# Clock-keeping products into unread accumulator columns, small loads later, and a new order of steps, in an attention and gated-MLP kernel

## Chip, cores, metric

One core of a Trainium2 chip. The metric is the device time of one execution in microseconds (us), lower is better. Engines: PE is TensorE, PEld its weight loads, DVE VectorE, ACT ScalarE, POOL GpSimd, SP SyncE.

## The reference, cut to what matters

```python
# q, k, v: 4 batches, 8 heads, 768 positions, 64 wide
keep = is_sink(4 first keys) | (0 <= row - col < 128)
a = softmax(where(keep, q @ k.T / 8, -1e9))
x = heads side by side of a @ v                       # 4 x 768 x 512
h = gelu(x @ w_in); u, v = halves of h
v = (v - mean(v)) / sqrt(var(v) + 1e-6) * g_ln
out = x + (u * (w_sg @ v + b_sg)) @ w_out             # w_sg mixes positions
```

## The kernel before

A list of steps is worked off in order. A step records instructions for one engine; each engine runs its own in that order, and the recording layer adds the waits between engines. `TQ`, `TK` turn q and k on TensorE, `EQ`, `EK` copy them out of PSUM, `QK` makes scores, `EX` their exponentials, `MK` masks them, `AV` multiplies by v, `NR` normalizes; `XT`, `XE` turn x; `MU`, `MV` are the gated unit's two halves, `SP` the mixing over positions, `GT` and `GM` the gate, `OU`, `RA`, `ST` the output. Numbers are batch, head pair, part; a last letter names the engine (A, D, P). PSUM has two double buffers `sc` and four single ones `mm`, taken in turn.

```python
pre = [0]
def HM(n):                       # n constant products, before the next product
    pre[0] = n
def fresh(ring, key):
    t = ring.new(key)
    for _ in range(pre[0]):      # into the buffer just given out; result never read
        nc.tensor.matmul(t if ring is mm_ring else t[:, 0, :], iden, ks_sink[1][:, 0:512], ...)
    pre[0] = 0
    return t
def TQ(b, p):                    # by way of transposes(): fresh(mm_ring, ...), 12 turns into columns 0:384
    ...
def MK(b, p, g, e):              # D: P = P * mask on VectorE; P: two affine_selects on GpSimd
    ...
def GM(b, hf, dc, e):            # gate product on VectorE (D) or GpSimd (P), all in SBUF
    (nc.vector if e == "D" else nc.gpsimd).tensor_mul(gatedT[...], gtmp[b, hf, dc], uT[b][...])
```

The softmax here doesn't subtract the row's maximum and nothing guards it: scores larger than these inputs give would overflow.

Of the kernel before, what the change touches and what calls it, by code (L numbers as in the profile page):

```python
# [13 lines left out]


STEPS = """
ZERO IDEN LQ.0.0 LK.0.0 LQ.0.1 FILL LK.0.1 LC MASK LV.0.0 MASK0 CQ.0.0.A LQ.0.2 HM.7 TQ.0.0 CK.0.0.A LK.0.2 EQ.0.0.A
LV.0.1 HM.2 TK.0.0 TQ.0.1 EK.0.0.A VSK EQ.0.1.D LQ.0.3 HM.2 QK.0.0.1 QK.0.0.2 KS.0.0 EX.0.0.1 VSM.3 LK.0.3 TK.0.1
SK.0.0 LV.0.2 VSM.1 EK.0.1.D CV.0.0.P EX.0.0.2 HM.6 QK.0.0.0 MK.0.0.1.D LV.0.3 TQ.0.2 SX.0.0 QK.0.1.0 KS.0.1 EX.0.0.0
EQ.0.2.D TK.0.2 MK.0.0.2.P SK.0.1 EX.0.1.0 EK.0.2.D QK.0.1.1 LW.0 EX.0.1.1 MK.0.0.0 HM.1 QK.0.2.1 LW.1 KS.0.2 TQ.0.3  # L20
VSM.0 SX.0.1 QK.0.2.0 EQ.0.3.A LWS SK.0.2 MK.0.1.1.D TK.0.3 EX.0.2.1 AV.0.0.0 MK.0.1.0 LWO AV.0.0.1 EK.0.3.A NR.0.0.0
QK.0.2.2 MK.0.2.1.P SX.0.2 NR.0.0.1 EX.0.2.0 CV.0.2.D LQ.1.0 KS.0.3 EX.0.2.2 CV.0.3.D LK.1.0 HM.7 QK.0.3.0 SK.0.3
MK.0.2.0 EX.0.3.0 QK.0.3.1 LV.1.0 MK.0.2.2.D AV.0.2.0 EX.0.3.1 MK.0.3.0 QK.0.3.2 AV.0.2.1 CV.0.1.P NR.0.2.0 EX.0.3.2
QK.0.1.2 NR.0.2.1 SX.0.3 MK.0.3.1.P AV.0.1.0 EX.0.1.2 NR.0.1.0 MK.0.3.2.P HM.1 AV.0.3.0 XT.0.0 NR.0.3.0 MK.0.1.2.P
AV.0.3.1 XE.0.0.D XT.0.1 NR.0.3.1 LV.1.1 AV.0.1.1 XE.0.1.A VSM.2 XT.0.3 LQ.1.1 MU.0.0 XE.0.3.A NR.0.1.1 LK.1.1 XT.0.2
LV.1.2 GU.0.0 MV.0.0 LV.1.3 LG WT.1 LQ.2.0 XE.0.2.A WT.4 WE.1 WT.0 GV.0.0 LK.2.0 MV.0.1 WE.4 WE.0 BN.0.0 MV.0.2 GV.0.1
BN.0.1 MU.0.3 GV.0.2 TQ.1.0 BN.0.2 RS.0.1 GU.0.3 TQ.1.1 MU.0.2 EQ.1.0.A EQ.1.1.A NM.0.1 RS.0.2 TK.1.0 Z.0.0.A TK.1.1
Z.0.1.D Z.0.2.A WT.5 NM.0.2 CV.1.0.P EK.1.0.D MU.0.1 EK.1.1.A Z.0.4.D LV.2.0 GU.0.2 WE.5 WT.3 WT.2 Z.0.5.A CV.1.1.P
WE.3 QK.1.0.0 Z.0.3.A WE.2 LV.2.1 GU.0.1 SP.0.0.2 EX.1.0.0 LQ.2.1 TQ.1.2 GT.0.0.2 LK.2.1 SP.0.0.3 EQ.1.2.D GM.0.0.2.P
TK.1.3 GT.0.0.3 TQ.1.3 EK.1.3.A MK.1.0.0 TK.1.2 QK.1.1.0 EQ.1.3.A GM.0.0.3.D SP.0.0.0 CV.1.2.P EK.1.2.D EX.1.1.0  # L30
QK.1.1.1 CV.1.3.D LV.2.2 SP.0.1.1 EX.1.1.1 GT.0.0.0 MK.1.1.0 LV.2.3 QK.1.2.1 QK.1.2.2 MK.1.1.1.D SP.0.1.2 EX.1.2.1
LQ.3.0 KS.1.0 EX.1.2.2 LK.3.0 SP.0.0.1 GM.0.0.0.D GT.0.1.2 MK.1.2.1.P SK.1.0 GT.0.1.1 QK.1.1.2 GT.0.0.1 SX.1.0
QK.1.3.2 MK.1.2.2.P TK.2.0 EX.1.1.2 TK.2.1 AV.1.1.0 GM.0.1.2.D EK.2.0.A GM.0.0.1.D QK.1.0.1 NR.1.1.0 MK.1.1.2.P
AV.1.2.1 EK.2.1.A OU.0.0 EX.1.0.1 NR.1.2.1 CV.2.1.P AV.1.1.1 CV.2.0.A RA.0.0 MK.1.0.1.P SP.0.1.0 NR.1.1.1 EX.1.3.2
ST.0.0 LV.3.0 AV.1.0.0 GM.0.1.1.D MK.1.3.2.D TQ.2.2 QK.1.2.0 GT.0.1.0 LV.3.1 EQ.2.2.A QK.1.0.2 SP.0.1.3 NR.1.0.0
EX.1.2.0 GM.0.1.0.P XT.1.0 GT.0.1.3 EX.1.0.2 TK.2.3 MK.1.2.0 OU.0.2 XE.1.0.A MK.1.0.2.D EK.2.3.A AV.1.2.0 CV.2.2.P
RA.0.2 AV.1.0.1 NR.1.2.0 TQ.2.1 GM.0.1.3.P ST.0.2 TK.2.2 NR.1.0.1 EQ.2.1.A TQ.2.0 CV.2.3.P QK.1.3.1 EK.2.2.D EQ.2.0.A
QK.1.3.0 OU.0.3 LQ.3.1 EX.1.3.1 KS.2.0 LK.3.1 XT.1.2 EX.1.3.0 OU.0.5 RA.0.3 LV.3.2 MK.1.3.1.D ST.0.3 QK.2.1.1 XE.1.2.A
QK.2.1.2 LV.3.3 RA.0.5 TQ.2.3 EX.2.1.1 TK.3.1 MK.1.3.0 ST.0.5 AV.1.3.1 EX.2.1.2 EQ.2.3.D MK.2.1.1.P AV.1.3.0 QK.2.0.2
EK.3.1.A QK.2.0.0 NR.1.3.1 SK.2.0 CV.3.0.P EX.2.0.2 OU.0.1 NR.1.3.0 EX.2.0.0 MK.2.0.2.P XT.1.1 RA.0.1 QK.2.0.1 SX.2.0  # L40
QK.2.1.0 CV.3.1.P XE.1.1.D XT.1.3 EX.2.0.1 ST.0.1 OU.0.4 MK.2.1.2.D XE.1.3.A MK.2.0.0 MV.1.0 EX.2.1.0 MK.2.0.1.P
RA.0.4 ST.0.4 MK.2.1.0 AV.2.0.0 GV.1.0 MV.1.1 NR.2.0.0 TK.3.3 GV.1.1 TK.3.2 BN.1.0 TQ.3.2 TQ.3.3 EK.3.3.A MV.1.2
CV.3.2.P EQ.3.2.A EQ.3.3.D EK.3.2.A BN.1.1 CV.3.3.P MU.1.3 GV.1.2 AV.2.1.0 BN.1.2 GU.1.3 RS.1.1 MU.1.0 MU.1.1 GU.1.0
NM.1.1 RS.1.2 NR.2.1.0 Z.1.0.A Z.1.3.D MU.1.2 NM.1.2 Z.1.2.A Z.1.1.D Z.1.5.D GU.1.1 AV.2.1.1 Z.1.4.D GU.1.2 AV.2.0.1
NR.2.1.1 QK.2.3.1 QK.2.2.0 NR.2.0.1 SP.1.1.0 EX.2.3.1 SP.1.1.3 GT.1.1.0 GM.1.1.0.D SP.1.0.3 EX.2.2.0 GT.1.1.3
MK.2.3.1.P QK.2.3.0 GT.1.0.3 QK.2.2.1 SP.1.1.2 EX.2.3.0 GM.1.1.3.D GM.1.0.3.D MK.2.2.0 EX.2.2.1 SP.1.0.1 MK.2.3.0
SP.1.0.2 MK.2.2.1.P GT.1.1.2 GT.1.0.1 AV.2.3.0 GM.1.1.2.D QK.2.2.2 GT.1.0.2 GM.1.0.1.P QK.2.3.2 AV.2.2.0 EX.2.2.2
NR.2.3.0 SP.1.0.0 GM.1.0.2.P EX.2.3.2 NR.2.2.0 TQ.3.1 MK.2.2.2.P GT.1.0.0 XD.2.0 TK.3.0 EQ.3.1.A TQ.3.0 MK.2.3.2.D
AV.2.2.1 EK.3.0.A EQ.3.0.D GM.1.0.0.P QK.3.1.2 QK.3.1.1 EX.3.1.2 AV.2.3.1 NR.2.2.1 OU.1.1 EX.3.1.1 KS.3.0 QK.3.0.0
MK.3.1.2.P NR.2.3.1 QK.3.1.0 EX.3.0.0 OU.1.2 RA.1.1 XD.2.1 MK.3.1.1.D EX.3.1.0 OU.1.0 MK.3.0.0 QK.3.0.2 ST.1.1  # L50
QK.3.0.1 RA.1.0 EX.3.0.2 SK.3.0 SP.1.1.1 MK.3.1.0 ST.1.0 EX.3.0.1 RA.1.2 MK.3.0.2.P MU.2.1 SX.3.0 GT.1.1.1 ST.1.2
MK.3.0.1.D MV.2.0 GM.1.1.1.P GU.2.1 OU.1.4 GV.2.0 MV.2.1 RA.1.4 BN.2.0 ST.1.4 MV.2.2 GV.2.1 BN.2.1 MU.2.3 GV.2.2
OU.1.5 BN.2.2 RS.2.1 GU.2.3 MU.2.2 RA.1.5 RS.2.2 MU.2.0 GU.2.2 NM.2.1 ST.1.5 Z.2.2.D Z.2.0.A Z.2.3.D OU.1.3 Z.2.1.D
GU.2.0 NM.2.2 QK.3.2.1 Z.2.4.D Z.2.5.A QK.3.3.0 AV.3.1.0 RA.1.3 EX.3.3.0 AV.3.1.1 NR.3.1.0 ST.1.3 SP.2.0.2 NR.3.1.1
SP.2.1.3 GT.2.0.2 EX.3.2.1 MK.3.3.0 SP.2.1.1 GM.2.0.2.D MK.3.2.1.P GT.2.1.3 QK.3.2.0 GT.2.1.1 QK.3.3.1 EX.3.2.0
SP.2.0.0 GM.2.1.3.D GM.2.1.1.D EX.3.3.1 SP.2.0.3 MK.3.2.0 GT.2.0.0 MK.3.3.1.P AV.3.2.0 GT.2.0.3 AV.3.0.0 QK.3.2.2
NR.3.2.0 GM.2.0.3.P QK.3.3.2 AV.3.3.0 EX.3.2.2 NR.3.0.0 AV.3.0.1 EX.3.3.2 MK.3.2.2.P NR.3.3.0 SP.2.0.1 NR.3.0.1 XD.3.0
MK.3.3.2.P SP.2.1.0 GT.2.0.1 GM.2.0.0.D AV.3.2.1 GM.2.0.1.D AV.3.3.1 GT.2.1.0 OU.2.1 NR.3.2.1 GM.2.1.0.P NR.3.3.1
OU.2.2 RA.2.1 XD.3.1 OU.2.0 RA.2.2 SP.2.1.2 RA.2.0 ST.2.1 ST.2.2 ST.2.0 MU.3.0 GT.2.1.2 GM.2.1.2.P MV.3.0 GU.3.0
OU.2.4 GV.3.0 MV.3.1 RA.2.4 BN.3.0 ST.2.4 MV.3.2 GV.3.1 BN.3.1 OU.2.5 GV.3.2 MU.3.2 BN.3.2 RS.3.1 MU.3.1 GU.3.2 NM.3.1  # L60
RS.3.2 RA.2.5 Z.3.2.A MU.3.3 Z.3.0.D ST.2.5 Z.3.1.A NM.3.2 Z.3.3.D OU.2.3 Z.3.4.A Z.3.5.D GU.3.3 SP.3.1.0 RA.2.3
GU.3.1 ST.2.3 SP.3.1.3 GT.3.1.0 GM.3.1.0.P SP.3.0.0 GT.3.1.3 GM.3.1.3.D SP.3.0.2 GT.3.0.0 GM.3.0.0.D SP.3.1.1 GT.3.0.2
GM.3.0.2.D SP.3.1.2 GT.3.1.1 GM.3.1.1.P SP.3.0.3 GT.3.1.2 GM.3.1.2.D SP.3.0.1 GT.3.0.3 GM.3.0.3.P OU.3.5 GT.3.0.1
OU.3.3 GM.3.0.1.D RA.3.5 OU.3.2 RA.3.3 ST.3.5 OU.3.0 ST.3.3 RA.3.2 OU.3.4 ST.3.2 OU.3.1 RA.3.4 RA.3.0 ST.3.4 ST.3.0
RA.3.1 ST.3.1
"""


# [8 lines left out]
def kernel(  # L77
# [14 lines left out]
    nc = tc.nc  # L92
# [40 lines left out]
    mm_ring = Ring("mm", 4, [128, 512], F32, psum)  # L133
# [24 lines left out]
    ks_sink = [sb.tile([128, HP * (128 + ks_w)], BF16, name=f"ks_sink{i}") for i in range(2)]  # L158

    iden = sb.tile([128, 128], BF16, name="iden")  # L160
# [9 lines left out]
    b_bc = sb.tile([128, S], F32, name="b_bc")  # L170
# [2 lines left out]
    wsg_rows = wsg_gated.rearrange("p (t s) -> p t s", t=NT)  # L173
    gatedT = wsg_gated.rearrange("p (r c s) -> p r c s", r=3, c=KU)

    pre = [0]

    def HM(n):
        pre[0] = n

    def fresh(ring, key):
        t = ring.new(key)
        for _ in range(pre[0]):
            nc.tensor.matmul(t if ring is mm_ring else t[:, 0, :], iden, ks_sink[1][:, 0:512], start=True, stop=True)
        pre[0] = 0
        return t

    def psb(key):
        return mm_ring[key].bitcast(BF16)[:, 0:S].rearrange("p (t i) -> p t i", t=NT)
# [63 lines left out]
            nc.sync.dma_start(out=vs32[i:128:16, :, :], in_=v[:, :, i, :].rearrange("b h d -> h b d"))  # L253

    def LG():
        nc.sync.dma_start(out=g_sb, in_=moe_g_ln.rearrange("(c p) -> p c", p=128))
        return nc.sync.dma_start(out=b_bc, in_=moe_b_sg.partition_broadcast(128))


    def IDEN():  # L260
# [41 lines left out]
    def transposes(name, ring, b, p):  # L302
        src = ring[b, p // 2]
        fresh(mm_ring, (name, b, p))
        ps = psb((name, b, p))
        for t in range(NT):
            for hl in range(2):
                nc.tensor.transpose(ps[64 * hl:64 * hl + 64, t, :], src[:, 2 * (p % 2) + hl, t, :], iden)  # L308
# [221 lines left out]
    def ST(b, t):  # L530
        nc.sync.dma_start(out=out[b, 128 * t:128 * (t + 1), :], in_=ot[b, t])


    code = {f.__name__: f for f in (
        HM, LQ, LK, LV, CQ, CK, CV, LW, LWS, LWO, LC, LG, IDEN, FILL, MASK, MASK0, VSK, ZERO, VSM, TQ, TK, EQ, EK, KS, SK, SX, QK, EX,
        MK, AV, NR, XT, XE, XD, MV, GV, BN, RS, NM, Z, MU, GU, WT, WE, SP, GT, GM, OU, RA, ST)}
    holds = dict(h.split("<") for h in HOLDS.split())
# [43 lines left out]
```

## Time and profile before

| kernel before | value |
|---|---|
| runs beside the change | 167.67 to 170.52 us, median 168.33 |
| span of the profiled run | 165.8 us |
| first gated-unit product on TensorE | 29.28 us |
| first mixing product (SP) | 45.02 us |
| last output product ends | 161.31 us |
| time at half clock before the tail | up to 4.81 us, and 8.22 to 11.63 us |

A busy row counts time in which an engine has an instruction under way. PEclk is the granted TensorE clock in tenths. It shows full clock up to the first record (4.81 us here), but the pace tells otherwise: the first seven 512-column products take 3.01 us, 0.43 each, twice the 0.215 of later ones, so the clock is at half there too. "Half until" a time is read so. Two marks divide the run into three: opening up to the first gated-unit product, then batch 0's first unit up to the first mixing product, then the rest. The prediction shows the lines.

### The profile page before, as it was taken

The numbers are of one execution on the slowest core, as the hardware profiler recorded it, in microseconds if no ns is written. First come the engines' busy times: TensorE is split into PE (matmuls) and PEld (weight loads), VectorE is DVE, ScalarE is ACT, GpSimd is POOL, SyncE is SP. The second block draws the span as 40 slices with busy tenths as digits, with TensorE's granted clock in tenths as the row PEclk, the third lists the DMA queues.
The fourth block names the chain that finished last, engine by engine and source line by source line (L and its number), as shares of the span: only waits on it lengthen the run. The fifth ranks groups of instructions, "written<-read, shape, count | busy, mean of one in ns | idle before, by whom it ended". The sixth has DMA issues, their size and how long they took to land.

```text
span 165.8 us, 4047 instructions
## 1 busy us (share of the span) xinstructions
PE 154.3 (93%) x1630; PEld 90.2 (54%) x1630; DVE 131.8 (79%) x302; ACT 110.2 (66%) x132; POOL 90.4 (54%) x123
## 2 busy tenths in 40 slices
PE   5599698999899999999999999999999999999990
PEld 1253446656565677665666575545567654555530
DVE  4179979389889989987997999838999963888861
ACT  3748966949998886999879748966676404590000
POOL 8999679646896999895240394321216610212400
PEclk9959999999999999999999999999999999999999
DMA  4999999999999998799000005901110475111055
GB/s 160 199 201 255 207 210 210 203 291 218 252 244 243 261 217 267 106 240 315 10 6 0 0 4 95 255 34 63 63 63 4 95 88 211 53 65 63 0 190 190
DMA packets 23249, 24.26 MB, mean 146 GB/s; under 512 B 8000, under 2 KB 18496, under 8 KB 23232
## 3 DMA queue, kind: packets, MB, share of 16 engines
q0 software_dynamic: 12128, 14.94, 46.5%
q1 hardware_dynamic: 11104, 9.08, 18.5%
q8 instruction: 12, 0.20, 0.5%
q14 instruction: 5, 0.04, 0.1%
HBM read 24.81 MB, written 6.29 MB: 188 GB/s over the span
## 4 chain that ended last, share of the span: by engine, by line
PE 68%; DVE 2%; DVEq 0%; issue 0%
PE mm L507 19%; PE mm L524 12%; PE sc L444 9%; PE sc L486 9%; PE sc L358 6%; PE mm L308 5%; PE mm L398 3%; PE mm L404 2%; PE mm L408 2%; DVE P L373 1%; PE mm L427 1%; PE mm L344 1%; DVEq L576 0%; DVE ot L528 0%; DVE gtmp L512 0%
## 5 line engine op out<-in xcount | busy, mean ns | idle before, releaser
L366 ACT ACTIVATE P<-sc 128x1024 bf16<-128x1024 f32 (+1 forms) x48 | 44.2, 968 | 10.8 <-PE sc L358 10.7
L507 PE MATMUL mm<-wsgT,z 128*128 128x384 bf16 x192 | 33.9, 327 | 0.7 <-DVE wsgT L502 0.7
L377 POOL TENSOR_SCALAR_AFFINE_SELECT P<-P 128x512 bf16<-128x512 bf16 x21 | 14.1, 669 | 23.0 <-ACT P L366 22.8
L507 PEld LDWEIGHTS <-z 128*128 128x128 bf16 x192 | 17.9, 98 | 13.4 <-issue 2.5
L528 DVE TENSOR_TENSOR ot<-mm,x_sb 128x512 f32<-128x512 f32 x24 | 16.3, 688 | 9.0 <-PE mm L524 8.8
L524 PE MATMUL mm<-w_out_sb,wsg_gated 128*128 128x512 bf16 x96 | 23.4, 380 | 0.0
L512 DVE SCALAR_TENSOR_TENSOR gtmp<-mm,g_sb,b_bc 128x384 bf16<-128x384 f32 x32 | 19.2, 613 | 4.4 <-PE mm L507 2.8
L486 PE MATMUL sc<-xT,w_in_sb 128*128 128x384 bf16 x128 | 22.6, 326 | 0.0
L444 PE MATMUL sc<-w_in_sb,xT 128*128 128x512 bf16 x96 | 22.2, 380 | 0.0
L373 DVE TENSOR_TENSOR P<-P,mask 128x1024 bf16<-128x1024 bf16 (+1 forms) x27 | 18.9, 718 | 1.4 <-ACT P L366 1.3
L517 POOL TENSOR_TENSOR wsg_gated<-gtmp,uT 128x384 bf16<-128x384 bf16 x13 | 12.9, 998 | 12.9 <-DVE gtmp L512 11.6
L492 ACT ACTIVATE uT<-sc 128x768 bf16<-128x768 f32 x16 | 12.7, 807 | 10.4 <-PE sc L486 10.4
L199 POOL DMA_DIRECT2D v<-in_v_dram x16 | 17.0, 1064 | 4.2 <-DVE gtmp L512 1.4
L418 DVE TENSOR_TENSOR x_sb<-mm,rcp 128x384 bf16<-128x384 f32 x32 | 17.8, 558 | 1.1
L448 ACT ACTIVATE vt<-sc 128x1024 f32<-128x1024 f32 x12 | 12.3, 1025 | 8.5 <-PE sc L444 7.7
L457 DVE BATCH_NORM_STATS2 st<-vt 128x6 f32<-128x512 f32 x24 | 16.2, 674 | 2.1 <-ACT vt L448 2.0
L465 POOL TENSOR_TENSOR rs<-rs,neg_half 128x4 f32<-128x4 f32 (+1 forms) x8 | 6.9, 864 | 19.4 <-DVE rs L460 17.5
L486 PEld LDWEIGHTS <-w_in_sb 128*128 128x128 bf16 x128 | 12.3, 98 | 8.4
L398 PE MATMUL mm<-v_sb,P 128*128 128x65 bf16 x192 | 16.4, 194 | 0.2 <-DVE P L373 0.2
L398 PEld LDWEIGHTS <-P 128*128 128x128 bf16 x192 | 14.3, 98 | 4.1 <-issue 1.5
L358 PE MATMUL sc<-qT,kT 64*128 64x256 bf16 x192 | 15.5, 269 | 0.1
L404 PE MATMUL mm<-v_sb,P 128*128 128x65 bf16 x160 | 15.4, 194 | 0.0
(75 smaller groups left out, 255.1 us busy)
## 6 DMA issues: line engine op xcount, KB each, us to landing
v<-in_v_dram POOLq DMA_DIRECT2D x16, 384.0 KB, 9.6
out_dram<-ot SPq DMA_DIRECT2D x24, 256.0 KB, 2.4
q<-in_q_dram POOLq DMA_DIRECT2D x6, 384.0 KB, 11.4
k<-in_k_dram POOLq DMA_DIRECT2D x6, 384.0 KB, 12.4
wsg_gated<-in_moe_w_sg_dram POOLq DMA_DIRECT2D x1, 1152.0 KB, 14.8
w_in_sb<-in_moe_w_in_dram POOLq DMA_DIRECT2D x2, 512.0 KB, 9.0
q<-in_q_dram POOLq DMA_DIRECT2D x3, 192.0 KB, 7.0
k<-in_k_dram POOLq DMA_DIRECT2D x3, 192.0 KB, 7.4
```

Source lines behind the costliest of these rows:

```text
L199: return nc.gpsimd.dma_start(out=ring.new((b, p)).rearrange("p h t d -> p (h t) d"), in_=src[b, 2 * p:2 * p + 2].rearrange("h (t p) d -> p ...
L358: nc.tensor.matmul(sc[:, hl, 256 * jl:256 * jl + n], kT[b, p][rows, 128 * j:128 * (j + 1)], qT[b, p][rows, 128 * j:128 * j + n], start=Tru ...
L366: nc.scalar.activation(out=pt[:, :, 0:w], in_=sc_ring[b, p, g][:, :, 0:w], func=AF.Exp, scale=scale)
L373: nc.vector.tensor_mul(pt[:, :, 0:w], pt[:, :, 0:w], m.unsqueeze(1).to_broadcast([128, 2, w]))
L398: nc.tensor.matmul(av[:, il, hl, :], P[b, p, i // 2][:, hl, 256 * (i % 2):256 * (i % 2) + 128], vb[:, h, i, :], start=first, stop=False)
L404: nc.tensor.matmul(av[:, il, hl, :], P[b, p, j // 2][:, hl, 256 * (j % 2) + 128:256 * (j % 2) + 256], vb[:, h, j, :], start=False, stop=False)
L418: nc.vector.tensor_mul(xs[:, 3 * half:3 * half + 3, 128 * p:128 * (p + 1)].rearrange("p t (h d) -> p t h d", h=2), av[:, :, :, 0:Dh], rcp. ...
L444: nc.tensor.matmul(hp[:, jl, :], xT[b][:, j, c, :], w_in_sb[:, c, d_half:2 * d_half], start=(c == 0), stop=(c == KD - 1))
L486: nc.tensor.matmul(hp[:, n, 0:NH], w_in_sb[:, c, 128 * dc:128 * (dc + 1)], xT[b][:, 3 * hf:3 * hf + 3, c, :], start=(c == 0), stop=(c == K ...
L507: nc.tensor.matmul(ps[:, 0:NH], z[b][:, si, 128 * dc:128 * (dc + 1)], wsgT[:, si, NH * hf:NH * (hf + 1)], start=(si == 0), stop=(si == NT ...
L512: nc.vector.scalar_tensor_tensor(out=gtmp.new((b, hf, dc)), in0=mm_ring["g", b, hf, dc][:, 0:NH], scalar=g_sb[:, dc:dc + 1], in1=b_bc[:, N ...
L524: nc.tensor.matmul(ps, gatedT[:, (2 * b + hf) % 3, dc, 128 * tl:128 * (tl + 1)], w_out_sb[:, dc, :], start=(dc == 0), stop=(dc == KU - 1))
```

## The change

Intent: keep the clock up with short products in columns 390 to 511, which readers of most buffers don't touch, so that no product has to wait for a buffer; move two small preparations later; order the steps anew. The order also puts other steps on other engines: 11 of 32 gate products go from VectorE to GpSimd.

```diff
-    pre = [0]
+    whole = set()                       # buffers whose readers use all 512 columns
     def HM(n):
-        pre[0] = n
+        i = (mm_ring.used - 1) % len(mm_ring.tiles)      # the newest buffer
+        while i in whole:
+            i = (i - 1) % len(mm_ring.tiles)
+        for _ in range(n):
+            nc.tensor.matmul(mm_ring.tiles[i][:, 390:512], iden, ks_sink[1][:, 0:122], start=True, stop=True)
... (fresh only keeps `whole` up to date)
     def LG():
-        nc.sync.dma_start(out=g_sb, ...)
-        return nc.sync.dma_start(out=b_bc, ...)
+        first = nc.sync.dma_start(out=b_bc, ...)
+        nc.sync.dma_start(out=g_sb, ...)
+        return first
... (STEPS: all 66 lines differ; pieces of batch 0's opening and of its gate)
-CQ.0.0.A LQ.0.2 HM.7 TQ.0.0 CK.0.0.A LK.0.2 EQ.0.0.A LV.0.1 HM.2 TK.0.0 TQ.0.1 EK.0.0.A
+CQ.0.0.A LQ.0.2 MASK0 HM.35 TQ.0.0 CK.0.0.D LK.0.2 EQ.0.0.A HM.10 TK.0.0 LV.0.1 EK.0.0.A HM.3 TQ.0.1 EQ.0.1.D LQ.0.3 HM.6
...
+GT.0.0.3 GM.0.0.2.P SK.1.0 EQ.2.1.D QK.1.1.1 SX.1.0 TK.2.1 GM.0.0.3.P EX.1.1.1 TK.2.0 AV.1.0.1 MK.1.1.2.D EK.2.1.A
+EK.2.0.D GM.0.0.1.P AV.1.0.0 ...
```

## The prediction

> **What bounds the kernel now.** I read the engine shares first, then the slices, then the chain of work that ended last, then TensorE's timeline.
>
> ```profile
> PE 154.3 (93%) x1630; PEld 90.2 (54%) x1630; DVE 131.8 (79%) x302; ACT 110.2 (66%) x132; POOL 90.4 (54%) x123
> PE   5599698999899999999999999999999999999990
> PEclk9959999999999999999999999999999999999999
> DMA  4999999999999998799000005901110475111055
> PE 68%; DVE 2%; DVEq 0%; issue 0%
> ```
>
> TensorE is the engine of the kernel: 93% busy, 68% of the last chain. Its gaps lie in the first ten or so slices and in the tail. In the third slice the granted clock falls to half. The DMA engines are full from slice 2 to slice 17, so the first 70 us are also a loading phase.
>
> A busy PE need not be at its pace, so I counted. Paces come from undisturbed pieces of the chain: four 512-column products 0.86 us, eighteen 384-column ones 2.93 us, twelve 64-wide transposes 0.46 us, six 128-wide ones 0.34 us. From 45.0 to 160.5 us the groups hold 192 products of line 507 (31.2), 94 of 524 (20.3), 96 of 486 (15.6), 72 of 444 (15.5), 240 q/k transposes (9.1), 24 of x (1.4), 264 window products at 0.030 and 48 sink products at 0.06 (10.8), 140 score products (about 8.5) and the sink scores (1.0): 113.4 us of work in 115.5 us. Only some 2 us are hidden loss there; 0.7 of them is the wait for a turned weight at 45.0 us. The same count for 0 to 45 us gives 27.4 us of useful work, so 17.6 us are lost in the opening, and the tail after the last product is 4.5 us. A new order can win or lose in the opening and hardly anywhere else.
>
> ```profile
> 2.06 3.01 PE L184 MATMUL mm<-ks_sink,iden 128*128 128x512 bf16 x7 [2.06 <-DVE ks_sink L293]
> 8.35 0.85 PE L308 MATMUL mm<-iden,q 128*64 128x128 bf16 x12 [1.01 <-DMA q<-in_q_dram]
> 9.13 1.03 PE L184 MATMUL sc<-ks_sink,iden 128*128 128x512 bf16 x2
> 10.10 0.93 PE L358 MATMUL sc<-qT,kT 64*128 64x256 bf16 x8
> 11.95 1.46 PE L184 MATMUL sc<-ks_sink,iden 128*128 128x512 bf16 x6
> 20.99 1.67 PE L184 MATMUL sc<-ks_sink,iden 128*128 128x512 bf16 x7 [1.54 <-ACT P L366]
> 29.28 1.46 PE L486 MATMUL sc<-xT,w_in_sb 128*128 128x384 bf16 x8
> 45.02 1.14 PE L507 MATMUL mm<-wsgT,z 128*128 128x384 bf16 x6 [0.73 <-DVE wsgT L502]
> 8.00:12.00 4.00, 3.65 (x36) 1.96 (x37) 2.64 (x6) 1.43 (x3) 3.64 (x5) 0.57 1.11 196
> ```
>
> Line 184 is the constant product, whose result nobody reads: 26 of them, 8.5 us busy, there to keep the clock up. The twelve transposes at 8.35 us take 0.78 us to the next row where others take 0.46: the clock is at half (0.57 in the window row). The exponentials set the pace of this stage, and the six products at 11.95 us and seven at 20.99 us stand before scores that ScalarE waits for (0.81 and 1.39 us idle there). The first gated-unit product starts at 29.28 us; from there TensorE is full.
>
> **What the Trainium skill says.** "TensorE: Matmul & The Clock Gate", Part 1, says that the clock is half until a free-running window of 3.4 us was busy, and half again after an idle one. The trace agrees in shape: one stretch of about 3.4 us at half clock begins near 8.4 us. Its window before held about 1.65 us of busy PE, much of it transposes, which Part 4 of that page says do not count as busy the same way. The same page's "Back-to-back issue gap" gives N/2.4 + 2.5 ns: 53 ns for 122 columns, 216 for 512; the trace has 57 for 128-wide transposes and 0.86/4 = 215. "PSUM — Partial Sum Buffer", section "PSUM bank collisions raise a hardware error", says two engines must not touch one bank and quadrant at once, disjoint columns or not. A program kept safe in that way must make a product in unread columns wait for the bank's reader. No wait of before's trace shows this, but the built program of the changed kernel does.
>
> **The change, part by part.** (1) 26 products of 512 columns become 155 of 122, in 19 groups, all in batch 0. At full clock 26 × 0.216 = 5.6 us become 155 × 0.057 = 8.8 us; the first 35 run mostly at half clock (0.10 each), 2.06 to about 5.35 us where the first seven ended at 5.0: the first transpose comes 0.35 us later.
>
> (2) They are meant never to wait. In the built program nine of the 18 later groups do (80 products), because they go into the newest buffer, and where its emptying step stands earlier in the list the group waits for that step:
>
> ```
> 10 before TK.0.0   : ACT copies q0      5 before AV.0.1.1 : ACT copies k3
>  3 before TQ.0.1   : ACT copies k0      6 before XT.0.0   : DVE empties XT.0.2
>  6 before QK.0.0.2 : DVE copies q1      5 before AV.0.2.0 : ACT empties XT.0.0
> 18 before QK.0.0.0 : DVE copies k1     10 before AV.0.3.0 : DVE normalizes AV.0.2.0
>                                        17 before XT.0.1   : DVE normalizes AV.0.3.0
> ```
>
> Before, a group waited for a buffer used two or four places ago. What stands behind a group now pays the newest evacuation and then the group. I walked the opening by hand with durations of the trace (copy on ScalarE 0.79, on VectorE 0.94, exponential 0.88 from start to start, sink exponential 0.5, mask 0.6 to 0.7, normalization 0.7). First q copy done at 6.68 (before: 7.46, as ScalarE no longer casts k); ten products to 7.27; TK.0.0 to 7.73; its copy to 8.63 (before 8.18); three products, TQ.0.1 8.8 to 9.3; VectorE's copy to 10.34; six products; scores at 10.7 (before 10.1), exponential at 11.1 (before 10.75). The 18 products wait until 13.05 for k1 and end at 14.1: third exponential at 14.4 (before 13.77). The cast of v1, now ScalarE's, adds 0.7; exponential 0.2.0 comes at about 20.5 (before 19.88), with one sink exponential fewer done. Then the last links: XT.0.0 held to 24.9, its copy 26.0, AV.0.2.0 to 26.7, normalized 27.4, ten products 28.0, AV.0.3.0 28.4, normalized 29.1, seventeen products 30.1, XT.0.1 30.5, two more AV halves: gated-unit products at about 31.6. That is 2.3 us later than 29.28. The largest terms are 17 × 0.057 = 0.97 and 10 × 0.057 = 0.57 at the end, wholly on the path.
>
> (3) Gate scales (2 KB in four-byte pieces, landing in 7.3 us beside the first loads) come behind the bias, after 31 us; two of the three early sink-row steps (0.9 us each with their cast) leave VectorE before 17 us. Worth a few tenths there; counted in the walk.
>
> (4) New order and engines: VectorE loses 11 gate products (0.34 each) to GpSimd (1.0 each), and gains masks, normalizations and casts: about 3 us more for VectorE, about 1 less for ScalarE, none over TensorE. In the full stretch this can recover part of the 2 us of hidden loss; I take 0.5. At the end, the last gate product is GpSimd's behind SP.3.1.0, with two output products (1.72) to hide 0.1 + 0.62 + 0.1 + 1.0 us: about 0.15 lost.
>
> Sum: +2.3 − 0.5 + 0.15 = about +1.9; taken a little smaller, 1.7, as the filled clock may save part: 168.97 + 1.7 = 170.7 us.
>
> **Rivals.** (a) The groups fill gaps that exist anyway, and the clock stays up. For it: without the nine waits the same walk reaches the gated unit at 26.7 us, 2.5 us sooner, so 166.5. Against: those waits are in the program, and earlier arrival meets loads (batch 1's first q, issued at 20.08, needs 16.2 us, so lands at 36.3, and the DMA row is full). (b) The half-clock window stays, since the new narrow groups between 5.0 and 8.4 us are only 0.9 us without transposes: one more us, 171.7 to 172.5. (c) Nothing happens: opening losses come from loads, and the rest is TensorE's own work; 168 to 169.5. For it: the count of 113.4 in 115.5. Against: ScalarE's idle spots above follow products, not loads. (d) The new order breaks the full stretch, say by GpSimd's slow gate products: 172 to 174. Nothing in the profile speaks for more than a few tenths, as GpSimd is 54% busy.
>
> **Range and chances.** Runs of before spread from 167.69 to 170.52, which is the phase of the clock's window, I think. Rivals (a) and (d) bound the range: 167.0 to 174.0. Faster than 165.6 needs more than all I find without waits: 0.10. Slower than 172.3 needs my walk plus (b) or (d): 0.26. Rest 0.64.
>
> **What would show it.** Right: constant products after the first group with waits on ScalarE or VectorE ahead of them, at k1, AV.0.2.0's and AV.0.3.0's normalizations; the first gated-unit product at 31 to 32 us; from there to the last product the same 131 us within 1. Wrong: no such waits, gated unit before 29 us; or the same gated-unit time and a stretch after it that is shorter by over 1 us; or a half-clock stretch that moved elsewhere.

## The result, and the profile after

The change takes 179.87 us median (179.42 to 180.35, 4 runs) against 168.33 us (167.67 to 170.52, 4 runs). The ratio is 1.0695, 95% interval 1.0635 to 1.0756: 7% slower, far above the range. Ratios here are the mean of one kernel's fast runs over that of the other's in the same rounds, so not quite the ratio of the medians.

The page of the changed kernel, first lines, slices and last chain:

```profile
span 178.7 us, 4292 instructions
PE 159.5 (89%) x1748; PEld 100.2 (56%) x1759; DVE 136.4 (76%) x302; ACT 110.2 (62%) x131; POOL 91.5 (51%) x121
PE   5667987699999975999999999999999999999970
PEclk9955899999999999999999999999999999999997
PE 79%; DVE 8%; ACT 5%; issue 4%; DMA 2%; DVEq 0%
```

TensorE now has gaps in the first eight slices, the fifth aside, and again in slices 15 and 16. The clock is at half in slices 3 and 4 and partly in 5. Work of VectorE and ScalarE has entered the last chain (8% and 5%, before 2% and none).

TensorE's timeline in the opening, the rows of the constant products (line 183) that waited, with the releaser in brackets, then the two marks:

```profile
7.23 0.69 PE L183 MATMUL mm<-ks_sink,iden 128*128 128x122 bf16 x10 [0.89 <-ACT qT L226]
9.27 0.40 PE L183 MATMUL mm<-ks_sink,iden 128*128 128x122 bf16 x3 [0.89 <-ACT kT L226]
11.50 0.77 PE L183 MATMUL mm<-ks_sink,iden 128*128 128x122 bf16 x6 [1.06 <-DVE qT L228]
15.49 1.99 PE L183 MATMUL mm<-ks_sink,iden 128*128 128x122 bf16 x18 [1.06 <-DVE kT L228]
...
33.16 0.69 PE L183 MATMUL mm<-ks_sink,iden 128*128 128x122 bf16 x10 [0.61 <-DVE x_sb L424]
35.09 1.07 PE L183 MATMUL mm<-ks_sink,iden 128*128 128x122 bf16 x17 [0.88 <-DVE x_sb L424]
...
37.46 1.46 PE L492 MATMUL sc<-xT,w_in_sb 128*128 128x384 bf16 x8
...
54.15 2.12 PE L513 MATMUL mm<-wsgT,z 128*128 128x384 bf16 x12
```

Each group waited for the step (a copy, or a normalization L424) that empties the buffer filled just before it, although that step reads other columns: the steps that the prediction read off the built program. The other three of its nine groups wait 0.56, 0.66 and 0.62 us, at 25.63, 29.79 and 31.49 us. Eighteen products took 1.99 us, 0.11 each, because the clock was at half. The gated unit starts at 37.46 us, 8.2 us later than before. Windows cut along the clock's own steps, with TensorE's busy time first and PEclk third from the end, the changed kernel and then the one before:

```profile
5.96:9.38 3.42, 1.64 (x37) 1.40 (x33) 0.58 (x2) 1.60 (x2) 3.42 (x6) 1.00 1.20 234
9.38:12.79 3.41, 2.35 (x29) 1.65 (x27) 1.71 (x4) 0.04 (x1) 3.41 (x5) 0.50 1.21 235
12.79:16.21 3.42, 2.36 (x28) 1.79 (x26) 1.73 (x4) 1.97 (x3) 0.88 (x2) 0.50 1.15 251
16.21:19.62 3.41, 3.41 (x36) 2.40 (x33) 0.29 (x2) 1.33 (x2) 0.00 (x0) 0.50 1.16 203
```

```profile
4.81:8.22 3.41, 1.78 (x27) 0.84 (x26) 0.00 (x0) 2.28 (x4) 3.34 (x7) 1.00 1.09 196
8.22:11.63 3.41, 3.28 (x34) 1.80 (x34) 2.27 (x5) 0.88 (x1) 3.05 (x4) 0.50 1.13 188
18.46:21.87 3.41, 1.86 (x30) 1.17 (x26) 3.31 (x8) 3.19 (x5) 2.96 (x5) 1.00 1.24 210
```

Both lose the clock after a window that is about half busy (1.64 and 1.78 of 3.41 us). Before gets it back after one window that is 96% busy. In the changed kernel two windows at 69% do not bring it back; the third, fully busy, does. After its first rise the clock is at half three times as long as before (10.24 against 3.41 us). That the waits of the products did this is tested by e2.

The second new gap is in the middle. VectorE, GpSimd and TensorE in the changed kernel around 63 us, one fence each:

```profile
62.10 0.95 DVE L228 COPY qT<-mm 128x768 bf16<-128x768 bf16 x1
62.97 4.69 DVE L379 TENSOR_TENSOR P<-P,mask 128x768 bf16<-128x768 bf16 x1
67.58 0.94 DVE L228 COPY kT<-mm 128x768 bf16<-128x768 bf16 x1
```

```profile
61.65 2.65 POOL L523 TENSOR_TENSOR wsg_gated<-gtmp,uT 128x384 bf16<-128x384 bf16 x3
64.25 0.63 POOL L383 TENSOR_SCALAR_AFFINE_SELECT P<-P 128x512 bf16<-128x512 bf16 x1
...
66.84 0.41 POOL L387 TENSOR_SCALAR_AFFINE_SELECT P<-P 128x256 bf16<-128x256 bf16 x1
67.21 1.06 POOL L204 DMA_DIRECT2D v<-in_v_dram  x1
```

```profile
68.58 1.14 PE L513 MATMUL mm<-wsgT,z 128*128 128x384 bf16 x6 [2.64 <-DVE kT L228]
```

One mask takes 4.69 us, where the masks of before mean 718 ns and none takes over 1.26 us. The group on the page of before, and its slowest case: two masks (the second takes the 1.26 us), with GpSimd's rows beside them:

```profile
L373 DVE TENSOR_TENSOR P<-P,mask 128x1024 bf16<-128x1024 bf16 (+1 forms) x27 | 18.9, 718 | 1.4 <-ACT P L366 1.3
62.51 1.89 DVE L373 TENSOR_TENSOR P<-P,mask 128x1024 bf16<-128x1024 bf16 x2
62.60 1.30 POOL L224 TENSOR_SCALAR v_sb<-v 128x768 bf16<-128x768 f32 x1
63.87 1.28 POOL L517 TENSOR_TENSOR wsg_gated<-gtmp,uT 128x384 bf16<-128x384 bf16 x1
```

The changed kernel's long mask ends 0.45 us after GpSimd leaves an unbroken run of work (61.65 to 67.25 us) for the issue of a load. The copy ahead of it, which reads PSUM, kept its 0.95 us under the same run. The Trainium skill, "SBUF — State Buffer", section "Who interferes with whom", says that a VectorE instruction with two SBUF inputs contends with GpSimd instructions that read SBUF, and that the loser is blocked, not slowed. The trace agrees, and the experiments below test it.

### The profile page after: what moved, and what is told of

Read it like the earlier page. It is cut to its first block, busy times and chain, and to the rows that moved or that the text cites. A ratio compares the mean times of both kernels' runs of the same rounds, so it can differ in the third digit from the quotient of the medians.

```text
span 178.7 us, 4292 instructions
## 1 busy us (share of the span) xinstructions
PE 159.5 (89%) x1748; PEld 100.2 (56%) x1759; DVE 136.4 (76%) x302; ACT 110.2 (62%) x131; POOL 91.5 (51%) x121
## 4 chain that ended last, share of the span: by engine, by line
PE 79%; DVE 8%; ACT 5%; issue 4%; DMA 2%; DVEq 0%
PE mm L513 16%; PE sc L450 11%; PE sc L492 11%; PE mm L530 10%; PE mm L183 7%; PE mm L314 7%; PE sc L364 6%; PE mm L404 3%; PE mm L410 2%; DMA out_dram<-ot 2%; PE mm L414 2%; DVE x_sb L424 2%; PE mm L433 1%; ACT kT L226 1%; ACT qT L226 1%
## 5 line engine op out<-in xcount | busy, mean ns | idle before, releaser
L523 POOL TENSOR_TENSOR wsg_gated<-gtmp,uT 128x384 bf16<-128x384 bf16 x24 | 23.8, 1001 | 22.5 <-DVE gtmp L518 21.1
L379 DVE TENSOR_TENSOR P<-P,mask 128x1024 bf16<-128x1024 bf16 (+1 forms) x30 | 26.1, 887 | 0.2
L530 PE MATMUL mm<-w_out_sb,wsg_gated 128*128 128x512 bf16 x91 | 22.8, 379 | 0.4 <-issue 0.2
L183 PE MATMUL mm<-ks_sink,iden 128*128 128x122 bf16 x155 | 14.8, 257 | 9.3 <-DVE ks_sink L299 2.1
L383 POOL TENSOR_SCALAR_AFFINE_SELECT P<-P 128x512 bf16<-128x512 bf16 x18 | 12.5, 692 | 16.7 <-ACT P L372 16.6
L183 PEld LDWEIGHTS <-iden 128*128 128x128 bf16 x155 | 12.3, 118 | 11.5 <-issue 9.6
L424 DVE TENSOR_TENSOR x_sb<-mm,rcp 128x384 bf16<-128x384 f32 x32 | 17.8, 558 | 1.1
L404 PE MATMUL mm<-v_sb,P 128*128 128x65 bf16 x192 | 16.3, 194 | 0.3 <-DVE x_sb L424 0.3
```

The lines of the kernel that those rows point to most:

```text
L183: nc.tensor.matmul(mm_ring.tiles[i][:, 390:512], iden, ks_sink[1][:, 0:122], start=True, stop=True)
L379: nc.vector.tensor_mul(pt[:, :, 0:w], pt[:, :, 0:w], m.unsqueeze(1).to_broadcast([128, 2, w]))
L404: nc.tensor.matmul(av[:, il, hl, :], P[b, p, i // 2][:, hl, 256 * (i % 2):256 * (i % 2) + 128], vb[:, h, i, :], start=first, stop=False)
L424: nc.vector.tensor_mul(xs[:, 3 * half:3 * half + 3, 128 * p:128 * (p + 1)].rearrange("p t (h d) -> p t h d", h=2), av[:, :, :, 0:Dh], rcp. ...
L523: (nc.vector if e == "D" else nc.gpsimd).tensor_mul(gatedT[:, (2 * b + hf) % 3, dc, :], gtmp[b, hf, dc], uT[b][:, dc, NH * hf:NH * (hf + 1)])
L530: nc.tensor.matmul(ps, gatedT[:, (2 * b + hf) % 3, dc, 128 * tl:128 * (tl + 1)], w_out_sb[:, dc, :], start=(dc == 0), stop=(dc == KU - 1))
```

## The experiments

All edits are to the changed kernel unless said. "Gated unit" is the start of the first gated-unit product in the profiled run, "mixing" that of the first mixing product. All results are correct except the one made wrong. The experiments came in three calls, each on another chip and with its own runs of before. Medians are of all runs; of these, two of e3 and two of e4 count as slow (over 1.5% above the fastest of their kernel), and one each of e8 and e10.

| kernel | median us (runs) | ratio to before | gated unit | mixing |
|---|---|---|---|---|
| before | 168.33 (4) | 1 | 29.28 | 45.02 |
| change | 179.87 (4) | 1.0695 | 37.46 | 54.15 |
| e1 no products | 171.72 (4) | 1.0206 | 27.40 | 45.36 |
| e2 oldest buffer | 171.79 (4) | 1.0213 | 29.08 | 45.77 |
| e3 gates on VectorE | 175.50 (4) | 1.0334 | 37.62 | 54.32 |
| e4 narrow products in before | 170.68 (4) | 1.0066 | 29.87 | 45.61 |
| e5 e1 and e3 | 167.19 (6) | 0.9962 | 26.70 | 45.23 |
| e6 e5 with first group | 167.24 (6) | 0.9954 | 27.45 | 45.43 |
| e7 before, no products | 170.73 (4) | 1.0163 | 32.51 | 48.24 |
| e8 before, small loads later | 168.45 (6) | 1.0010 | 27.72 | 44.54 |
| e9 one product a group | 177.65 (4) | 1.0582 | 33.88 | 51.59 |
| e10 mask behind the copy | 171.63 (4) | 1.0196 | 27.64 | 46.36 |
| e11 e5, root before load | 166.65 (6) | 0.9939 | 27.06 | 43.87 |
| e12 mask reads nothing | 167.99 (1, wrong) | none | 26.28 | 46.28 |

**e1: no products.**

```diff
-        for _ in range(n):
+        for _ in range(0):
```

> The changed kernel without any constant product. Theory W (the products wait for the newest buffer's emptying, which delays what stands behind them and leaves TensorE too idle to get its clock back): the waits vanish, the clock may stay at half for long in the opening; the first gated-unit product comes earlier than 37.5 us, at 32 to 36 us, and the kernel takes 174 to 178 us. Rival O (the new order itself is bad in the opening, whatever the products do): first gated-unit product at 37 us or later, 179 to 182 us.

171.72 us, better than either theory said. The gated unit comes 10 us sooner than with the products and 1.9 us sooner than in the kernel before, although the clock is at half until 16.6 us. So the new order is good in the opening and the products spoil it; the rival falls. (Against the old order without products, e7 below, it is 5.1 us sooner.) The 4.69 us mask is still there, and after the gap behind it the clock falls to half for one window, as the last of these window rows shows:

```profile
59.00:61.00 2.00, 1.14 (x6) 0.58 (x6) 1.93 (x5) 0.00 (x0) 0.48 (x1) 1.00 0.38 106
61.00:64.40 3.40, 3.22 (x44) 2.38 (x44) 3.37 (x8) 1.50 (x2) 2.14 (x3) 0.50 0.17 53
```

**e2: the same products in the buffer emptied longest ago.**

```diff
-        i = (mm_ring.used - 1) % len(mm_ring.tiles)
+        i = mm_ring.used % len(mm_ring.tiles)
         while i in whole:
-            i = (i - 1) % len(mm_ring.tiles)
+            i = (i + 1) % len(mm_ring.tiles)
```

> The same 155 products at the same places, but written into the buffer that will be given out next (emptied longest ago) instead of the newest. Theory W: no wait ahead of the first five groups, half clock for at most one window of 3.4 us, first gated-unit product at 27 to 31 us, kernel 169 to 173 us. Rival O: first gated-unit product still after 35 us, kernel 177 us or more.

171.79 us and 29.08 us, as the theory had it:

```profile
29.08 1.46 PE L492 MATMUL sc<-xT,w_in_sb 128*128 128x384 bf16 x8
```

The clock stays whole from 4.95 us to the middle stall. Same number of products, same places, another buffer: 8 us. So the target buffer, and with it the waits, is what made the products so dear. But with the clock up the kernel is no faster than with no products and half clock: the products' own time costs 1.7 us at the gated unit (29.08 against 27.40).

**e3: three gate products of batch 0 back on VectorE.**

```diff
-GM.0.0.2.P ... GM.0.0.3.P ... GM.0.0.1.P
+GM.0.0.2.D ... GM.0.0.3.D ... GM.0.0.1.D
```

> The changed kernel with three gate products of batch 0 moved from GpSimd back to VectorE (0.3 us each there). Theory P (the mask that took 4.69 us at 63 us was held off by GpSimd's unbroken run of work[...]): that mask takes under 2 us, the idle 2.6 us of TensorE at 66 us go, kernel 176 to 178 us (2 to 4 us less than the change). Rival D (VectorE was simply late, or the time comes back elsewhere): 179 to 181 us.

175.50 us median, 4.4 us less; the runs spread from 172.97 to 177.80 and two of four count as slow, the profiled one (176.26) among them. The two fast runs, 172.97 and 174.75 us, are 6.0 us below the change, so the size is rough. The same mask in VectorE's timeline:

```profile
63.67 0.55 DVE L379 TENSOR_TENSOR P<-P,mask 128x768 bf16<-128x768 bf16 x1
```

The gap of TensorE is gone; GpSimd is idle when the mask starts. Theory P holds so far; the size is a little above it.

**e4: narrow products in the kernel before.**

```diff
 # before, with HM and fresh of the change, and each count times 512/122:
-HM.7 ... HM.2 ... HM.2 ... HM.6 ... HM.1 ... HM.7 ... HM.1
+HM.29 ... HM.8 ... HM.8 ... HM.25 ... HM.4 ... HM.29 ... HM.4
```

> The kernel before with its own order and places, but its 26 products of 512 columns replaced by 109 of 122 columns (equal columns in all) into the newest buffer, as the change does it. Theory W: six groups now wait for the newest emptying, so the opening gets longer by 2 to 6 us: 170.5 to 175 us. Rival O: the products' new target costs nothing, 167.5 to 169.5 us.

168.14 to 171.94 us, ratio 1.0066 (0.998 to 1.015, from two fast runs of four): not told apart from before, though the median, which counts the two slow runs, is in the theory's range. The edit makes 107 products, not 109. The waits are there (0.83 us ahead of the 29 products at 20.46 us, for a normalization), but the gated unit is only 0.6 us late, and the profiled run, the fastest of the four, has no half-clock window after its first rise (6.52 us). Perhaps in the old order a group stands where TensorE would have waited anyway; that is not shown. Inconclusive for time.

**e5: no products, and the gates on VectorE** (the edits of e1 and e3).

> The changed kernel without any constant product and with the three gate products of batch 0 on VectorE. The two losses found so far should add: the mask that took 4.69 us in the kernel without products (171.7 us) takes under 1 us, TensorE's 2.6 us gap and the one window of half clock behind it go, so 171.7 - 2.6 - 1.7 = 167.4 us, 166.5 to 168.5 us, about even with the kernel before (168.1). Rival S (something else in the new order still costs, behind those two): 169.5 us or more.

167.19 us, ratio 0.9962 (0.9909 to 1.0016), where 167.4 was worked out: the two losses add, the mask at that place takes 0.55 us, and with both gone the rest of the change is level with the kernel before. What is left open in it is a gap of TensorE at 40.84 us, used in e11.

**e6: the first group kept**, on top of e5.

```diff
-        for _ in range(n):
+        for _ in range(n if n == 35 else 0):
```

> As the kernel without products and with the gate products on VectorE, but the first group of 35 products, which waits for no reader, stays. Theory C (half clock until 16.6 us costs something in the opening that products ahead of the first transpose can save): first gated-unit product before 27.0 us, kernel 0.3 to 1.5 us below that without any. Rival N (the opening is paced by ScalarE and VectorE, so the clock hardly matters there, and one window later it is half anyway): within 0.3 us of it, or slower since the first transpose comes 0.5 us later.

167.24 us: the same as e5, as rival N said. But this says little of what the clock is worth, since its clock was at half for about as long as e5's (until 6.75 and from 13.58 to 16.99 us, against until 10.45). The kept profiles say more: e5, e11, e12, e1 and e10, all without products and with all but the same opening, have half clock until 10.45, 13.39, 14.83, 16.61 and 18.18 us, and the gated unit at 26.70, 27.06, 26.28, 27.40 and 27.64 us. In this order, nearly 8 us more of half clock go with about 1 us.

**e7: the kernel before without products.**

```diff
-        pre[0] = n
+        pre[0] = 0
```

> The kernel before without its 26 products. Theory W' (products in front of waiting work cost more than the clock they keep): the two ScalarE idle spots before the delayed scores shrink, first gated-unit product at 27.5 to 29 us, kernel 166.5 to 168 us. Rival C' (they pay for themselves by the clock): 168.5 to 171 us.

170.73 us, 1.0163 (1.0099 to 1.0227). My theory W' falls and the rival holds: in the old order the products do pay. Without them the clock is at half until 10.7 us, from 14.1 to 20.9 and from 24.3 to 31.2 us, and the gated unit comes at 32.51 us. That the clock is the cause fits these times; why the old order needs it and the new one hardly does was not tried further.

**e8: the kernel before with the small preparations later.**

```diff
-    EX.0.0.1 VSM.3 ... VSM.1 EK.0.1.D ... VSM.0 SX.0.1 ... VSM.2 XT.0.3
+    EX.0.0.1 VSM.0 ... EK.0.1.D ... SX.0.1 ... VSM.2 VSM.1 VSM.3 XT.0.3
 (and LG as in the change)
```

> The kernel before with one part of the change alone: gate scales loaded behind the bias, and the sink rows of batches 1 to 3 made after batch 0's attention. Theory: a few tenths in the opening at most, 167.4 to 168.4 us, no difference that three or five rounds show. Rival: the small pieces among the first loads hold the q, k, v loads up by a microsecond, 166 to 167.3 us.

168.45 us, 1.0010 (0.9941 to 1.0079). That part of the change is worth nothing that shows.

**e9: one product in each group.**

```diff
-        for _ in range(n):
+        for _ in range(1 if n < 35 else 0):
```

> The changed kernel without its first group and with one product in each of the other 18 groups: the nine waits for the newest buffer stay, the products' own time nearly goes. To be held against the kernel without products (171.7 us, first gated-unit product 27.4 us) and the change (179.9 us, 37.5 us). Theory V (the waits are the larger part): first gated-unit product at 32 to 36 us, kernel 176 to 180 us. Rival Q (the 155 products' own time on the path is the larger part): first gated-unit product at 28 to 30 us, 172 to 174 us.

177.65 us and 33.88 us: theory V. Eighteen products of a few hundredths of a microsecond each, with their nine waits, cost 5.9 us against no product. What the other 137 products add to reach the change is 2.2 us (179.87 − 177.65). The clock is low here too (half until 18.9, and 29.1 to 35.9 us), so the 5.9 us hold waits and the clock lost by them together. e10, further down, helps to part them: without products, its clock was at half nearly as long at first (until 18.18 us), and its gated unit came at 27.64 us, 6.2 us sooner. From 29.11 to 33.88 us only e9 was at half, with TensorE busy for 3.69 us; at twice the pace that would be at most 1.8 us less. So, as an estimate from these two profiles, some 4 us of the 6.2 come of the groups and their waits even with the clock at half in both.

**e10: the long mask one place later**, on top of e1.

```diff
-MK.1.1.2.D EK.2.1.A EK.2.0.D
+EK.2.1.A EK.2.0.D MK.1.1.2.D
```

> The kernel without products (171.7 us), with the mask that took 4.69 us one place later on VectorE, behind the copy of a k that TensorE waits for; the gate products stay on GpSimd. Theory P (the mask is held until GpSimd pauses): the copy, which reads PSUM, ends about 4 us sooner in normal time, the mask starts about 0.9 us later and still ends when GpSimd turns to a load, so takes 3.5 to 4 us; TensorE's 2.6 us gap shrinks or moves to a later product, kernel 169 to 171 us. Rival D (VectorE as such is slow or late there): the copy is long or late too, and the time stays within 0.5 us of 171.7.

The instructions do what theory P says. VectorE's timeline, then GpSimd's:

```profile
55.61 0.96 DVE L228 COPY kT<-mm 128x768 bf16<-128x768 bf16 x1 [0.35 <-PE mm L314]
56.48 3.39 DVE L379 TENSOR_TENSOR P<-P,mask 128x768 bf16<-128x768 bf16 x1
```

```profile
59.05 0.41 POOL L387 TENSOR_SCALAR_AFFINE_SELECT P<-P 128x256 bf16<-128x256 bf16 x1
59.42 1.07 POOL L204 DMA_DIRECT2D v<-in_v_dram  x1
```

The copy runs at once in normal time, the mask starts later and again ends 0.45 us after GpSimd turns to its load. The time, 171.63 us (169.73 to 173.26), misses what I expected, and lies where rival D put it, though D's long or late copy is not there: TensorE's wait went to the next link, an AV product that waits 2.20 us at 61.32 us for a normalization behind the mask. It had been named as possible, and took nearly the whole gain.

**e11: the inverse root before a waiting load**, on top of e5.

```diff
-NR.0.2.1 LK.2.0 MU.0.0 ... BN.0.2 RS.0.1 GU.0.2
+NR.0.2.1 MU.0.0 ... BN.0.2 RS.0.1 LK.2.0 GU.0.2
```

> The kernel without products and with the gate products on VectorE (167.2 us), in which GpSimd takes batch 0's first inverse root before the issue of a k load of batch 2, which waits for an earlier load to land. Theory: the 1.43 us gap of TensorE before a q transpose at 40.8 us, which followed that root, shrinks to under 0.5 us, kernel 165.5 to 166.6 us, faster than both. Rival: the later load or another wait takes its place, 166.9 to 167.5 us.

In e5 TensorE had this gap, first fence; GpSimd's row that led to it is in the second, an issue that waits for a landing while the root stands behind it:

```profile
40.84 0.53 PE L314 MATMUL mm<-iden,q 128*64 128x128 bf16 x12 [1.43 <-DVE wsgT L508]
```

```profile
37.69 0.75 POOL L201 DMA_DIRECT2D k<-in_k_dram  x1 [1.49 <-DMA k<-in_k_dram]
38.45 1.73 POOL L471 TENSOR_TENSOR rs<-rs,neg_half 128x4 f32<-128x4 f32 x2
```

In e11 that gap is gone, mixing starts at 43.87 us instead of 45.23, and the kernel takes 166.65 us (six runs, 165.78 to 167.47), just above the expected range. Against the kernel before it is 0.9939 (0.9889 to 0.9990): the fastest here, by about 0.6%. Against e5, the difference is within the noise.

**e12: the long mask reads nothing**, wrong (relative error 0.46), on top of e1.

```diff
+            if (b, p, g) == (1, 1, 2):
+                nc.vector.memset(pt[:, :, 0:w], 0.0)
+                return
```

> Wrong result on purpose: the kernel without products (171.7 us), with the mask that took 4.69 us replaced by a fill with zeros of the same block, which reads nothing; all else and GpSimd's work unchanged. Theory P (the reads are what is held): the fill takes under 0.6 us and the 2.6 us gap goes, one run of 167 to 169 us. Rival D (VectorE is stopped as a whole while GpSimd works, or its write is held): the fill is as long as the mask was, 171 to 172 us.

```profile
55.02 0.38 DVE L379 MEMSET P<- 128x384 uint32 x1
55.35 0.96 DVE L228 COPY kT<-mm 128x768 bf16<-128x768 bf16 x1
```

The fill takes 0.38 us, under the same GpSimd run (53.6 to 59.2 us here), and the copy follows at once. One run of 167.99 us, state unknown, in the range. Reading from SBUF was what was held; VectorE was not stopped, nor was its write. Whether one SBUF input would have been held like two, no run tells apart.

## Why the prediction was wrong

The direction and the first mechanism were right. Two steps failed: the walk of the opening, +2.3 us where 8.2 were measured, and the new order's −0.5 us with its harmless gate products on GpSimd, which cost some 4.5 us. In all it was +11.5 us in place of +1.7.

1. *Nine groups wait for the newest evacuation*: right, and shown. The waits named at k1 and at the two normalizations stand in the trace with 1.06, 0.61 and 0.88 us, and no other of the later groups waits.
2. *The walk of the opening, +2.3 us*: this term failed. It was 8.2 us (37.46 − 29.28). From the runs, one profile of each, it splits into −1.9 for the order without products (e1), +6.5 for the groups with their waits and the clock lost by them (e9 over e1), and +3.6 for the bulk of the products (the change over e9). I had walked at the full clock and on single links; what I missed is that the waits also empty TensorE's windows, and after two at 69% busy it was still at half. That is not all of it. Laid against the trace, the walk is 0.6 us too early at the end of k0's copy (9.22 us, walked 8.63), 3.7 at the third exponential (18.06, walked 14.4), 5.0 at exponential 0.2.0 (25.48, walked 20.5) and 5.9 at the gated unit (walked 31.6). Some 3 us of this came while the clock was at half; the last 2 came mostly after it was back at 19.62 us, and which links they belong to stays open. With the buffer changed (e2) the clock stays up and the gated unit comes at 29.08 us.
3. *Rival (b), one more us at half clock*: right in kind, too small; I counted how busy the window before would be and not the two after it. (In before, cut along the clock's steps, that window holds 1.78 us of busy TensorE, not 1.65.) Nor do the traces bear out my use of the skill's Part 4, that transposes count for less: in e10 the window from 38.66 to 42.07 us held 1.79 us of busy TensorE, all but 0.13 of it transposes, and the clock stayed full; e7 lost it after 1.83 us without a single transpose (20.91 to 24.32).
4. *Rival (a)'s 26.7 us without waits*: e5 and e1 have 26.70 and 27.40 us, but with no products at all. With the products and without these waits it is 29.08. And an earlier gated unit did not carry through: e5 is 2.6 us ahead at the gated unit and 0.2 behind at the mixing, partly because the list turns two more q pairs first, partly through a gap of 1.43 us behind a load issue on GpSimd (e11).
5. *The new order recovers 0.5 us in the full stretch; nothing speaks for rival (d) as GpSimd is 54% busy*: failed. Three of the eleven gate products moved to GpSimd cost 4.5 us (e5 against e1), or 4.4 to 6.0 (e3, by all or by fast runs). The share of busy time said nothing: what counted was one run without a pause beside a VectorE instruction that reads SBUF. I had costed the moved products by their own durations only.
6. *Small preparations later, a few tenths*: right, nothing to be seen (e8).
7. *Same 131 us from the gated unit to the last product*: it was 132.0 before (161.31 − 29.28) and 135.5 after (172.92 − 37.46), the difference being mainly point 5: with the three gates back on VectorE (e3) it is 132.3.
8. *The spread of before as the phase of the clock's window*: only a guess, and not borne out by the granted clocks. A run of before with 169.93 us shows 1.000 after its first rise, and one with 167.03 us 0.994.

The medians along one path: e11 166.65; e5 167.19; gates on GpSimd, e1 171.72; one product a group, e9 177.65; all products, the change 179.87.

Open: the exact shares of waiting and half clock in e9's 5.9 us, since no kernel had the waits with the clock held; why GpSimd's run shut the mask out here and not in before at 63 us; and why the old order depends on the clock (e7) and the new one hardly does (the profiles under e6).

## What to carry to other kernels

A filler that is meant to wait for nothing has to go where no reader is still at work, which is the buffer emptied longest ago, not the newest one; look in the built program at what it waits for, and test first whether the fillers pay at all. A wait on TensorE can cost more than its length if it drops the busy share of a clock window. Before moving work to an idle-looking GpSimd, look at which VectorE instructions with two SBUF inputs will run beside it, and look at a mask's length in the trace; whether pauses left on purpose help was not tried.

## What the Trainium skill lacked or had wrong

- "SBUF — State Buffer", "Who interferes with whom": it says that whoever issues first has the shared pair for the whole instruction. Here VectorE's mask was kept out across a whole run of seven GpSimd instructions, 4.69 or 4.70 us in four profiles (the change, e1, e2, e9; 62.97 to 67.66 us in the change) and 3.39 us in e10, with no turn shown for it between two of them; each time it ended about 0.45 us after GpSimd turned to issuing a load. No page says that an unbroken run can hold VectorE that long, nor when a turn comes: in before, a mask that began at 63.13 us under four GpSimd instructions without a pause (61.71 to 65.96 us) was through after 1.26 us, 0.49 us after one of them had ended.
- "TensorE: Matmul & The Clock Gate", Part 1: it gives a busy window as what releases the clock and an idle one as what takes it, and says that frequent short idle times can make it swing, but gives no share. Here full clock was lost after windows 48% and 52% busy (1.64 and 1.78 of 3.41 us) and 54% (1.83, e7), kept after 55% (1.86, before) and 53% (1.79, e10, 38.66 to 42.07 us), so in these traces it goes at about half. It was not given back after two at 69% (2.35 and 2.36) nor after 92% (3.15, e10, 7.94 to 11.35 us), but was after 96% (3.28), and at the start of before after 81% (2.75, 1.39 to 4.81 us), so the busy share alone does not settle when it comes back.
- "PSUM — Partial Sum Buffer", on collisions: its rule by bank fits the nine waits seen here, 0.56 to 1.06 us for readers of other columns; nothing to add.
